# Staged weight loads, gathers and weight pieces put in another order between attention and the experts

## The chip, the cores and the metric

One core of a Trainium2 chip runs the whole program. The metric is device time in microseconds (us) of one execution; smaller is better. The time of the kernel before is the median of three runs.

Five engines work side by side[...]: TensorE (PE in the profile, PEld for its weight loads), VectorE (DVE), ScalarE (ACT), GpSimd (POOL) and SyncE (SP). SyncE and ScalarE issue plain DMA transfers here; GpSimd issues the indirect ones (gathers and scatters by a list of row numbers) and those that convert fp32 to fp16 on the way.

## The reference

Two layers, one behind the other. The first is causal linear attention with decay, in blocks of 64 positions, for 4 batches x 8 heads x 768 positions x 64. Its output is the input of the second, seen as 3072 tokens of 512 numbers. The second sends each token to the one of 8 experts whose embedding is nearest to it by cosine.

```python
xn = x / (np.linalg.norm(x, axis=-1, keepdims=True) + 1e-06)
en = expert_emb / (np.linalg.norm(expert_emb, axis=-1, keepdims=True) + 1e-06)
logits = xn @ en.T / tau
expert_idx = np.argmax(logits, axis=1)
...
for e in range(E):
    mask = expert_idx == e
    h = np.maximum(x[mask] @ w1[e], 0.0)            # [n, 512] @ [512, 1024]
    out[mask] = gate_w[mask, None] * (h @ w2[e])    # [n, 1024] @ [1024, 512]
```

`gate_w` is the softmax probability of the chosen expert. Each expert has 4 MB of fp32 weights, so the experts together read 32 MB.

## The kernel before

**Attention** runs in 24 blocks of 128 tokens, `for i in range(1, R)`. As blocks finish, they are routed in seven groups: of four blocks each for the first five, then of two. A routed group is written row by row to a table in DRAM, `x_dram`, by `write_x`. From the routing the kernel makes lists of the rows of each *region*. Regions 0 and 1 hold the first tokens (those of the first 16 blocks) of experts 0 and 1, regions 2 and 3 the rest of these two, regions 4 to 9 all tokens of experts 2 to 7. A region has 1, 2 or 3 full tiles of 128 tokens and a half tile of 64; the half tiles of two neighbouring regions share one gather, called `("h", r)`.

**The experts.** For each tile of a region the rows are gathered from `x_dram` to `x_e` by GpSimd, transposed by PE into PSUM (`xtr`), and copied to `xTe` by ScalarE. `pe_L1(r)` computes the hidden layer of region r in 8 groups of four matmuls, each followed by a relu on ScalarE. `pe_L2(r, g)` computes the output of one tile in eight matmuls (`pe_L2h(r)` that of two half tiles), and `put` scales it by the gate on VectorE and scatters it to the output by an indirect DMA.

```python
        def pe_xT(r, g0, g1):
            xt_copy(r, g0, g1, ps_mx.tile([P, DC * P * (g1 - g0)], FP16, name="xtr", tag="xtr"))
        ...
        def put(y_ps, r, g):
            y = moe_y.tile([P, DM], FP32, name="y_sb", tag="y_sb")
            nc.vector.tensor_scalar(y, y_ps, xe[r][:, g, DW : DW + 1].bitcast(FP32), None,
                                    op0=ALU.mult)
            nc.gpsimd.indirect_dma_start(
                out=out_views[n_scat[0]],
                ...)
            for x in after.get(n_scat[0], []):
                ...                       # the gathers of later regions, in a fixed order
            if n_scat[0] > 1:
                part_cast()
            n_scat[0] += 1
```

**The weights** come in two ways. Those of experts 0 to 2 come in twelve pieces that GpSimd's DMA converts to fp16 (`load_w`; 512 KB each as written, 1 MB as read). Those of experts 3 to 7 come in 40 *parts* of 512 KB of fp32: SyncE loads a part into one of four staging tiles (`w_st`), VectorE casts it to fp16 into the weight tile, and the next load starts into the tile that came free.

```python
        def part_load():
            if at_part[0] < len(parts):
                ...
                t = wst.tile([P, F], FP32, name="w_st", tag="w_st")
                nc.sync.dma_start(t, ...)
                staged.append(t)

        def part_cast():
            at_part[2] += 1
            if at_part[1] < len(parts) and at_part[2] % 5:
                ...
                nc.vector.tensor_copy(w..., staged.pop(0))
                part_load()
```

`part_cast` is called at fixed places: in `put` from the third output tile on, and inside `pe_L1`:

```python
            nc.scalar.activation(hT[r][:, fc, 0:n], h_ps[:, 0:n], AF.Relu)
            if r > 0 and fc % (4 if n < P * 2 else 2) == 1:
                part_cast()
```

Every fifth call does nothing. `n` is 320 tokens for regions 0 and 1, 192 for 2 and 3, and 448 for the others, so a hidden layer of region 1 or of 4 to 9 has four such calls, one of 2 or 3 has two.

**The hand-over.** In the attention loop, gathers and weight pieces are issued on GpSimd at the end of block i:

```python
    for i, r, g in ((19, 0, 0), (19, 0, 1), (20, ("h", 0), 0), (20, 1, 0), (20, 1, 1)):
        at(i, "g", gather, r, g)
    for i in (7, 9, 11, 13, 15, 19, 19, 20, 20, 21, 21, 21):
        at(i, "g", load_w, 1)
```

The first gathers need the row writes of the first four groups, that of the fourth (`write_x(3)`) being issued by ScalarE in block 19. After the last block:

```python
        write_x(GL)
        pe_L1(0, range(4, 8))
        for _ in range(4):
            part_load()
        for gi in range(GL - 2, GL + 1):
            pe_list(gi, kaz[:, 320:384], first=(gi == GL - 2), last=(gi == GL))
        ev_list(GL)
        ids(ES, NR)
        gather(2, 0)
        gather(3, 0)
        gather(pairs.pop(0), 0)
        rt_b2(GL)
        pe_L2(0, 0)
        pe_L2(0, 1)
        pe_L1(1)
        pe_L2h(0)
        pe_xT(2, 0, 1)
        pe_L2(1, 0)
        pe_xTh(2)
        pe_L2(1, 1)
        pe_L1(2)
        pe_xT(3, 0, 1)
        pe_L2(2, 0)
        pe_xT(4, 0, 2)
        pe_L1(3)
        pe_xT(4, 2, 3)
        pe_L2h(2)
        pe_xTh(4)
        pe_L2(3, 0)
        for r in range(2 * ES, NR, 2):
            ...                           # regions 4 to 9
```

Of the kernel before, what the change touches and what calls it, by code (L numbers as in the profile page):

```python
# [20 lines left out]
def kernel(  # L21
# [13 lines left out]
    P = 128  # L35
# [56 lines left out]
    moe_t1 = ctx.enter_context(tc.tile_pool(name="moe_t1", bufs=2))  # L92
    moe_h1 = ctx.enter_context(tc.tile_pool(name="moe_h1", bufs=1))
# [589 lines left out]

    todo = {}

    def at(i, slot, fn, *a):
        todo.setdefault((i, slot), []).append((fn, a))
# [26 lines left out]
    for i, r, g in ((19, 0, 0), (19, 0, 1), (20, ("h", 0), 0), (20, 1, 0), (20, 1, 1)):  # L714
        at(i, "g", gather, r, g)
    for i in (7, 9, 11, 13, 15, 19, 19, 20, 20, 21, 21, 21):
        at(i, "g", load_w, 1)

# [92 lines left out]
    def pe_L1(r, fcs=range(FC), early=()):  # L811
# [6 lines left out]
        for k, fc in enumerate(fcs):  # L818
            if early:
                h_ps = ps.tile([P, 512], FP32, name="s_h", tag=early[k])  # L820
            else:
                h_ps = ps_h.tile([P, 512], FP32, name="h_ps", tag="h")
            for c in range(DC):
                nc.tensor.matmul(h_ps[:, 0:n], w_chunk(w, c, fc), xTe[r][:, c, 0:n],  # L824
                                 start=(c == 0), stop=(c == DC - 1))
            nc.scalar.activation(hT[r][:, fc, 0:n], h_ps[:, 0:n], AF.Relu)  # L826
            if r > 0 and fc % (4 if n < P * 2 else 2) == 1:
                part_cast()
# [13 lines left out]
    with (  # L842
# [5 lines left out]
        tc.tile_pool(name="wst", bufs=4) as wst,  # L848
# [15 lines left out]

        parts = [(e, which, c) for e in range(3, E) for which in (1, 2) for c in range(DC)]
        staged = []
        at_part = [0, 0, 0]

        def part_load():
            if at_part[0] < len(parts):  # L870
                e, which, c = parts[at_part[0]]
                at_part[0] += 1
                t = wst.tile([P, F], FP32, name="w_st", tag="w_st")
                nc.sync.dma_start(t, w1_r[e][:, c, :] if which == 1
                                  else w2_r[e][:, c].rearrange("p s d -> p (s d)"))
                staged.append(t)

        def part_cast():
            at_part[2] += 1
            if at_part[1] < len(parts) and at_part[2] % 5:  # L880
                e, which, c = parts[at_part[1]]
                at_part[1] += 1
                w_alloc(e)
                w = w_tiles[(e, which)]
                nc.vector.tensor_copy(w[:, c, :] if which == 1  # L885
                                      else w[:, 2 * c : 2 * c + 2, :].rearrange("p s d -> p (s d)"),
                                      staged.pop(0))
                part_load()

        pairs = [("h", r) for r in range(ES, NR, 2)]  # L890

        def pe_xT(r, g0, g1):
            xt_copy(r, g0, g1, ps_mx.tile([P, DC * P * (g1 - g0)], FP16, name="xtr", tag="xtr"))

        def pe_xTh(r):
            xth_copy(r, ps_mx.tile([P, DC * P], FP16, name="xtr_h", tag="xtr"))

        def put(y_ps, r, g):
            y = moe_y.tile([P, DM], FP32, name="y_sb", tag="y_sb")
            nc.vector.tensor_scalar(y, y_ps, xe[r][:, g, DW : DW + 1].bitcast(FP32), None,  # L900
                                    op0=ALU.mult)
# [16 lines left out]
            if n_scat[0] == n_out - 8:  # L918
                nc.gpsimd.drain()
# [55 lines left out]
        for _ in range(4):  # L975
            part_load()
# [4 lines left out]
        gather(2, 0)  # L981
        gather(3, 0)
        gather(pairs.pop(0), 0)
# [4 lines left out]
        pe_L2h(0)  # L988
        pe_xT(2, 0, 1)
        pe_L2(1, 0)  # L990
        pe_xTh(2)
        pe_L2(1, 1)
        pe_L1(2)
        pe_xT(3, 0, 1)
# [138 lines left out]
```

## Time and profile before

| | |
|---|---|
| median of three runs | 259.68 us (259.17 to 264.58) |
| the profiled run | 264.65 us, of which 263.0 us are the program's span |
| busy share of the span | PE 92%, VectorE 53%, GpSimd 52%, ScalarE 47% |
| moved by DMA | 60.33 MB, mean 229 GB/s |

The profile gives for each engine when it worked, and for each idle time what ended it. A line of a group or of the timeline names the source line (L824), the engine, the operation, and the tiles as output<-input. L824 are the matmuls of the hidden layers, L826 the relus, L925 and L934 the matmuls of the output layers, L900 and L902 the scaling and the scatter of an output tile, L653 the gathers, L666 the transposes of gathered rows, L874 and L885 the staged load of a part and its cast, L321 and L323 the weight pieces of GpSimd, L462 the row writes. "x_e<-x_dram,lid" is a gather of a full tile, "x_e<-x_dram,lh" one of half tiles. A wait for several things is put down to the one that came last by the profile.

In the span, attention runs to about 133 us and the experts from 135 us to 257 us.

### The profile page before, as it was taken

To read this page: it belongs to the slowest core of one execution; us is meant where nothing else is said; L and a number is where in the kernel's file an instruction comes from. 1 tells how busy PE (TensorE), PEld (TensorE's weight loads), DVE (VectorE), ACT (ScalarE), POOL (GpSimd) and SP (SyncE) were. 2 spreads that over 40 slices of the span, in tenths; PEclk is the share of its full clock that TensorE was granted. 3 is DMA by queue.
4 is the path that set the end of the run, shared out by engine and by line. 5 is a ranking of instruction groups with operands and counts; after the bars stand their busy time and mean duration, and the time that the engine had idled before them with its cause. 6 is when DMAs were issued, how large, how long until landed. Compare 5 with 4: busy or idle time off the path is not lost. (4 is left out here: it accounts for less than half of the span.)

```text
span 263.0 us, 7404 instructions
## 1 busy us (share of the span) xinstructions
PE 241.4 (92%) x3011; PEld 166.8 (63%) x3012; DVE 139.1 (53%) x353; ACT 123.2 (47%) x277; POOL 137.2 (52%) x191
## 2 busy tenths in 40 slices
PE   7989999999999999989999864799999999999990
PEld 3777898897887987967855423475555555455440
DVE  1554677577667667846756524036554544554031
ACT  4745564653564555534573411355454436353600
POOL 7653436449236736269940877037274837440541
PEclk9999999999999999999999979599999999999997
DMA  7999999999999999339999999467898999982321
GB/s 152 238 223 231 238 207 228 253 242 196 210 198 249 228 229 238 85 61 216 198 226 270 340 358 337 182 196 215 327 319 303 310 393 332 306 284 90 128 83 57
DMA packets 79542, 60.33 MB, mean 229 GB/s; under 512 B 54504, under 2 KB 68840, under 8 KB 79506
## 3 DMA queue, kind: packets, MB, share of 16 engines
q1 hardware_dynamic: 71440, 42.51, 59.7%
q0 software_dynamic: 6976, 16.63, 26.2%
q10 hardware_dynamic: 1090, 0.70, 1.2%
q8 instruction: 24, 0.39, 0.6%
q14 instruction: 12, 0.10, 0.2%
HBM read 56.48 MB, written 10.94 MB: 256 GB/s over the span
## 5 line engine op out<-in xcount | busy, mean ns | idle before, releaser
L824 PE MATMUL h_ps<-xTe,w_sb 128*128 128x448 f16 (+2 forms) x312 | 52.6, 324 | 5.9 <-ACT hT L826 4.4
L826 ACT ACTIVATE hT<-h_ps 128x448 f16<-128x448 f32 (+2 forms) x78 | 36.9, 481 | 43.3 <-PE h_ps L824 27.3
L900 DVE TENSOR_SCALAR y_sb<-y_ps,x_e 128x512 f32<-128x512 f32 x29 | 21.7, 750 | 51.8 <-PE y_ps L925 22.8
L339 POOL TENSOR_TENSOR ks<-kn,kdec 128x512 f32<-128x512 f32 (+1 forms) x25 | 25.2, 1008 | 45.6 <-issue 20.7
L824 PEld LDWEIGHTS <-w_sb 128*128 128x128 f16 x320 | 30.6, 99 | 27.7 <-issue 7.4
L925 PE MATMUL y_ps<-w_sb,hT 128*128 128x512 f16 x192 | 47.3, 399 | 0.0
L392 DVE TENSOR_TENSOR stm<-s_ps,step 128x512 f32<-128x512 f32 x48 | 30.9, 686 | 26.4 <-PE s_ps L384 23.0
L902 POOL DMA_INDIRECT out_dram<-y_sb,lid x24 | 26.0, 1085 | 34.4 <-DVE y_sb L900 29.5
L653 POOL DMA_INDIRECT x_e<-x_dram,lid x24 | 26.2, 1092 | 16.3 <-PE h_ps L824 8.2
L885 DVE CAST w_sb<-w_st 128x1024 f16<-128x1024 f32 x40 | 27.5, 712 | 12.4 <-DMA w_st<-in_moe_w_dram 11.9
L925 PEld LDWEIGHTS <-hT 128*128 128x128 f16 x192 | 18.9, 102 | 21.2 <-issue 3.7
L384 PE MATMUL s_ps<-qT,kT 64*64 64x128 f32 x768 | 27.4, 276 | 0.9 <-issue 0.6
L415 PE MATMUL o_ps<-stm,vn 128*64 128x128 f32 x384 | 26.8, 279 | 0.2 <-issue 0.2
L456 ACT ACTIVATE sq<-xps 128x512 f16<-128x512 f32 x24 | 14.3, 598 | 24.3 <-PE xps L454 23.0
L384 PEld LDWEIGHTS s_ps<-qT,kT 64*64 64x64 f32 x768 | 21.2, 132 | 7.0 <-issue 5.3
L415 PEld LDWEIGHTS o_ps<-stm,vn 128*64 128x64 f32 x384 | 20.5, 136 | 3.1 <-issue 2.6
L424 ACT COPY xT<-o_ps 128x256 f32<-128x256 f32 x24 | 8.9, 373 | 28.1 <-PE o_ps L415 28.1
L360 DVE TENSOR_TENSOR qT<-q_ps,lamq 128x512 f32<-128x512 f32 x22 | 15.1, 687 | 3.5 <-PE q_ps L354 3.2
L674 ACT COPY xTe<-xtr 128x512 f16<-128x512 f16 (+1 forms) x14 | 10.8, 768 | 11.7 <-PE xtr L666 8.7
L370 PE MATMUL k_ps<-ident,ks 128*128 128x128 f32 x96 | 14.8, 275 | 0.8 <-POOL ks L339 0.7
L586 POOL TENSOR_SCALAR l_row<-lrow,hl 128x128 f16<-128x128 f32 x22 | 13.3, 603 | 4.1 <-DVE hl L547 3.8
L372 ACT COPY kT<-k_ps 128x512 f32<-128x512 f32 x24 | 14.4, 598 | 2.1 <-PE k_ps L370 2.1
(148 smaller groups left out, 335.9 us busy)
## 6 DMA issues: line engine op xcount, KB each, us to landing
w_st<-in_moe_w_dram SPq DMA_DIRECT2D x40, 512.0 KB
vn<-in_v_dram SPq DMA_DIRECT2D x24, 256.0 KB
w_sb<-in_moe_w_dram POOLq DMA_DIRECT2D x12, 512.0 KB
kn<-in_k_dram SPq DMA_DIRECT2D x23, 256.0 KB
qn<-in_q_dram SPq DMA_DIRECT2D x11, 512.0 KB
x_dram<-xg SPq DMA_DIRECT2D x8, 272.0 KB
x_dram<-xg ACTq DMA_DIRECT2D x2, 272.0 KB
x_dram<-xg SPq DMA_DIRECT2D x4, 136.0 KB
```

The lines of the kernel that those rows point to most:

```text
L339: nc.gpsimd.tensor_tensor(ks[i][:, h : h + n], kn[i][:, h : h + n], kdec[:, i % RB, h : h + n].unsqueeze(2).to_broadcast([P, n, D]), op=AL ...
L360: nc.vector.tensor_tensor(qT[j][:, :, :, s, :].rearrange("p a h i -> p h a i"), t.rearrange("p h (a i) -> p h a i", i=64), lamq[:, j % NC, ...
L384: nc.tensor.matmul(bank["s", h2][ds(64 * m, 64), hp, :], kT[i][ds(64 * h2, 64), hp, ds(64 * m, 64)], q_of(i, hp)[ds(64 * h2, 64)], start=( ...
L392: nc.vector.tensor_tensor(stm[i][:, h2], bank.pop(("s", h2)), step.unsqueeze(1).to_broadcast([P, HP, P]), op=ALU.mult)
L415: nc.tensor.matmul(bank["o", h2][ds(64 * u, 64), b2, :], vn[i][:, 2 * hp + h2, :], stm[i][:, h2, hp, :], start=(i % RB == 0 and b2 == 0), ...
L653: nc.gpsimd.indirect_dma_start(out=xe[r][:, g, :], out_offset=None, in_=x_dram[0 : TA * P] if first else x_dram[:], in_offset=bass.Indirec ...
L824: nc.tensor.matmul(h_ps[:, 0:n], w_chunk(w, c, fc), xTe[r][:, c, 0:n], start=(c == 0), stop=(c == DC - 1))
L826: nc.scalar.activation(hT[r][:, fc, 0:n], h_ps[:, 0:n], AF.Relu)
L885: nc.vector.tensor_copy(w[:, c, :] if which == 1 else w[:, 2 * c : 2 * c + 2, :].rearrange("p s d -> p (s d)"), staged.pop(0))
L900: nc.vector.tensor_scalar(y, y_ps, xe[r][:, g, DW : DW + 1].bitcast(FP32), None, op0=ALU.mult)
L902: nc.gpsimd.indirect_dma_start(out=out_views[n_scat[0]], out_offset=bass.IndirectOffsetOnAxis(ap=idl[r][:, 1, g : g + 1], axis=0), in_=y[: ...
L925: nc.tensor.matmul(y_ps, hT[r][:, fc, ds(col0(r) + P * g, P)], w[:, fc, :], start=(fc == 0), stop=(fc == FC - 1))
```

## The change

It reorders what shares the DMA engines around the hand-over, so that the gathers of the second regions (2 and 3) don't run beside weights, and uses the stretch in which little is moved:

- The first four staged loads go to the end of attention block 18. A memset of one column of each staging tile on VectorE holds them back until there: SyncE has to wait for it. The pool of staging tiles is made at the start of the kernel for that.
- The first half-tile gather goes from block 20 to block 19, and only five weight pieces are issued in blocks 20 and 21, instead of seven in blocks 19 to 21. The last two, of expert 2's second layer, are issued after the gathers of regions 2 and 3. These gathers come in the order region 2, half tiles, region 3.
- Region 1's hidden layer has no casts any more (`r > 1`), so that no further staged load starts before the third output tile.
- PE's order changes: the first output tile of region 1 comes before the transposes of region 2, and all transposes of regions 2 and 3 before the hidden layer of region 2.
- The transposes go by turns to two PSUM banks instead of one (`xt_bank`).
- The last output tile is scaled half by VectorE and half by ScalarE, and GpSimd's drain comes when seven output tiles are left instead of eight.

```diff
+    wst = ctx.enter_context(tc.tile_pool(name="wst", bufs=4))
...
+    def part_load():
+        if at_part[0] < len(parts):
...
+            t = wst.tile([P, F], FP32, name="w_st", tag="w_st")
+            if len(staged) < 4 and at_part[0] <= 4:
+
+                nc.vector.memset(t[:, 0:1], 0.0)
+            nc.sync.dma_start(t, w1_r[e][:, c, :] if which == 1
+                              else w2_r[e][:, c].rearrange("p s d -> p (s d)"))
+            staged.append(t)
...
-    for i, r, g in ((19, 0, 0), (19, 0, 1), (20, ("h", 0), 0), (20, 1, 0), (20, 1, 1)):
+    for i, r, g in ((19, 0, 0), (19, 0, 1), (19, ("h", 0), 0), (20, 1, 0), (20, 1, 1)):
         at(i, "g", gather, r, g)
-    for i in (7, 9, 11, 13, 15, 19, 19, 20, 20, 21, 21, 21):
+    for i in (7, 9, 11, 13, 15, 20, 20, 20, 21, 21):
         at(i, "g", load_w, 1)
+
+    for _ in range(4):
+        at(18, "end", part_load)
...
-            if r > 0 and fc % (4 if n < P * 2 else 2) == 1:
+            if r > 1 and fc % (4 if n < P * 2 else 2) == 1:
                 part_cast()
...
+        n_xt = [0]
+
+        def xt_bank(n):
+            n_xt[0] += 1
+            if n_xt[0] % 2:
+                return ps_mx.tile([P, n], FP16, name="xtr", tag="xtr")
+            return ps2.tile([P, n], FP16, name="xtr2", tag="xps")
...
+            gate = xe[r][:, g, DW : DW + 1].bitcast(FP32)
+            if n_scat[0] == n_out - 1:
+                nc.vector.tensor_scalar(y[:, 0 : DM // 2], y_ps[:, 0 : DM // 2], gate, None, op0=ALU.mult)
+                nc.scalar.activation(y[:, DM // 2 :], y_ps[:, DM // 2 :], AF.Copy, scale=gate)
+            else:
+                nc.vector.tensor_scalar(y, y_ps, gate, None, op0=ALU.mult)
...
-            if n_scat[0] == n_out - 8:
+            if n_scat[0] == n_out - 7:
                 nc.gpsimd.drain()
...
         pe_L1(0, range(4, 8))
-        for _ in range(4):
-            part_load()
...
         gather(2, 0)
+        gather(pairs.pop(0), 0)
         gather(3, 0)
-        gather(pairs.pop(0), 0)
+        load_w(2)
         rt_b2(GL)
         pe_L2(0, 0)
         pe_L2(0, 1)
         pe_L1(1)
         pe_L2h(0)
+        pe_L2(1, 0)
         pe_xT(2, 0, 1)
-        pe_L2(1, 0)
+        pe_L2(1, 1)
         pe_xTh(2)
-        pe_L2(1, 1)
+        pe_xT(3, 0, 1)
         pe_L1(2)
-        pe_xT(3, 0, 1)
         pe_L2(2, 0)
```

## The prediction

> **What bounds the kernel now.** I read the page's slices first. Slice n begins at n x 6.575 us. TensorE (PE) is at 9 tenths nearly everywhere but in slices 22 to 25 (145 to 171 us), the hand-over from attention to the experts; there alone its clock falls too. DMA is full from slice 18 on, with two holes: slices 16 and 17 (105 to 118 us) and 25 to 27.
>
> ```profile
> PE   7989999999999999989999864799999999999990
> ...
> PEclk9999999999999999999999979599999999999997
> DMA  7999999999999999339999999467898999982321
> ```
>
> So outside the hand-over the matmuls are the limit, and a microsecond saved inside it reaches the end if the stages behind can follow. The second view is busy time by windows (window, its length, busy us of PE, PEld, DVE, ACT, POOL with counts, granted clock, DMA share, GB/s).
>
> ```profile
> 152.00:154.00 2.00, 0.46 (x3) 0.00 (x0) 1.35 (x2) 0.00 (x0) 1.69 (x2) 1.00 0.90 266
> ...
> 156.00:158.00 2.00, 2.00 (x6) 0.72 (x5) 0.00 (x0) 0.00 (x0) 1.67 (x2) 0.51 1.02 416
> ...
> 162.00:164.00 2.00, 0.24 (x3) 0.24 (x3) 0.00 (x0) 0.33 (x1) 1.39 (x3) 1.00 0.89 325
> ...
> 168.00:170.00 2.00, 2.00 (x6) 0.76 (x5) 0.00 (x0) 0.46 (x1) 0.00 (x0) 0.50 0.05 21
> ```
>
> PE loses time in two ways, idle and at half clock. The third view, the timeline of this stretch, says which waits (start, duration, what, and in brackets the idle time before it and who ended it).
>
> ```profile
> 144.55 1.31 POOL L653 DMA_INDIRECT x_e<-x_dram,lid  x1 [8.22 <-PE h_ps L824]
> ...
> 147.50 1.05 POOL L653 DMA_INDIRECT x_e<-x_dram,lh  x1 [0.30 <-issue]
> ...
> 154.51 0.60 PE L666 MATMUL xtr_h<-ident,x_e 128*128 128x128 f16 x4 [2.05 <-DMA x_e<-x_dram,lh]
> ...
> 163.37 0.33 ACT L826 ACTIVATE hT<-h_ps 128x192 f16<-128x192 f32 x1 [3.24 <-remote]
> ...
> 163.75 0.49 PE L824 MATMUL h_ps<-xTe,w_sb 128*128 128x192 f16 x4 [3.08 <-ACT hT L826]
> ```
>
> The gather of region 2 starts at 144.55 although its list was ready at 140.8: the matmul named was long done, so what it waited for is the last row write (issued 139.41). That write shares the DMA engines with the tail of seven SWDGE weight pieces (share 1.11 over 130 to 140 us) and, from 140.73, with the first four staged loads. The gather then needs 5.8 us until PE starts on it (144.55 to 150.33, where PE waited 1.1 us for it), that of the half tiles 7.0 us (147.50 to 154.5), because L1(1)'s four casts have released four more 512 KB loads. PE idles, and runs at half clock after it. The third stall (160.7 to 166.2) is different: relus of L1(2) wait 3.2, 1.1 and 1.1 us for products whose matmuls were recorded earlier.
>
> [...] 0.51 and 0.50 above, and eight 512-column matmuls take 3.41 us from 154.90 against 1.89 at 150.57. [...]
>
> **The change, part by part.**
>
> *Four staged loads move* from 140.73 into the hole at 105 to 118 us. A memset behind block 18's router step (VectorE, done about 106.7) holds them until then. At 364 GB/s, the rate of 144.5 to 150 us, a 512 KB load takes 0.524/0.364 = 1.44 us, so four fill 5.8 us of a hole with share 0.35. They overlap the fourth group's row writes (issued 107.92, 108.64; the first gather waits for them until 113.47). I allow the gather 0 to 2 us of delay. Its transposes start at 119.29, and the tile waited for no DMA then; the two weight pieces that came between the first gathers are now behind them. Effect on the end: 0 to +1 us.
>
> *Weight pieces:* five instead of seven before the hand-over. Seven pieces ran from 117 to 140, some 3.2 us each beside the row writes, so five end about 6 us earlier and the last row write meets a freer DMA. I put the gather of region 2 at 142 to 143 instead of 144.55. The order is now region 2, half tiles, region 3, then the two pieces: half tiles at 144 to 145 instead of 147.50.
>
> *No casts in L1(1)* (r > 1), so no staged load starts before the third row-block eviction (about 150). The gathers have DMA to themselves; I give them 3 us instead of 5.8 to 7.
>
> *PE order:* L2(1,0) before xT(2), xT(3) before L1(2), transposes in two PSUM banks. From L2h(0) at 147.3 (full-clock durations from the timeline): L2h(0) 1.92 + L2(1,0), L2(1,1), L2(2,0) 3 x 1.89 + xT(2), xTh, xT(3) 3 x 0.40 + L1(2) 3.3 (as L1(3), 171.77 to 175.07) + xT(4,0:2) 0.61 = 12.7 us. ScalarE's two half copies before L1(2), 0.65, make 13.4. L1(3) would start at 160.7; it starts at 171.75 now. **That is 11 us to be had in the profiled run.** Data is there in time: region 2 is needed at 151.1 (landed by 146), half tiles at 153.4 (by 148), region 4's first two at 159.5. Those last come behind two pieces and two scatters at some 1.35 us per GpSimd issue, so about 151, plus 7 us at worst.
>
> *Last eviction split* over VectorE and ScalarE: half of 0.75, some 0.3 us off the tail.
>
> **How much of the 11 us the timed runs hold.** The profiled run took 264.65 us, the median of three 259.68. So 5 us of the profile are not in a median run. The third stall is the only one of about that size whose cause the trace doesn't show (160.7 to 166.2, plus half clock behind it); I assume that it is mostly what the median lacks. Then 11 - 5 = 6 us remain to be won; if the 5 us lie elsewhere, 11.
>
> **Can DMA follow?** It is the candidate for the next bound.
>
> ```profile
> 180.00:240.00 60.00, 60.00 (x365) 31.06 (x364) 30.16 (x49) 30.33 (x54) 30.63 (x33) 1.00 0.91 311
> 147.30:240.00 92.70, 83.98 (x526) 45.11 (x526) 41.21 (x65) 39.48 (x79) 47.92 (x49) 0.94 0.86 295
> ```
>
> From 147.3 to 240 DMA works 92.7 x 0.86 = 79.7 us. After the change one staged load fewer is left then (36 instead of 37: -1.4) and two SWDGE pieces more (+6.4): 84.7 us. At the 0.91 of the steady stretch this takes 93 us and ends at 146 + 93 = 239; at 0.97 it ends at 233. The last cast (240.9 now) is needed at L2h(8), 249.1 now and 238 after an 11 us shift. So loads and matmuls finish close together: casts come later against PE (four chances lost in L1(1), so the fortieth falls into L1(9) instead of before it), and VectorE, which also empties y_ps, will sometimes wait for w_st. I take 0 to 3 us for it, 1 in the middle.
>
> Sum for the median run: 259.7 - 6 (or up to -11) + 0.5 (attention) - 0.3 (tail) + 1 (loads). With the smaller saving 254.9, with the larger 249.9; at weights of about 0.6 and 0.4, **253.0 us**.
>
> **Rivals.** (a) Loads become the bound: the steady share of 0.91 and 8.8 us of casts waiting for w_st after 171.7 speak for it, PE's 60.00 of 60.00 in the same stretch against it: today's waits cost PE nothing. Then 255 to 258. (b) The early loads hold back the fourth group's row writes, thus the first gathers and the transposes in block 21, and attention stalls: for it, both use all DMA engines from 107 on; against it, 6 us between gather and use. Costs 1 to 3 us, so 254 to 256. (c) The third stall stays in L1(2), as its cause is open: DMA shares near 1 beside it speak for that, the lighter loads in the new order against it. Then 257 or so. (d) All goes well and the median has the whole 11 us: 249.
>
> **Range and chances.** 2% is 254.5. The middle of my sum lies 1.5 us below it, (a) and (c) lie above, (d) far below. Range 248.5 to 258.5. Faster by over 2%: 0.64; within 2%: 0.32; slower: 0.04, as no part adds more than 3 us to a path that loses at least 3.
>
> **What would show it.** Four w_st loads between 106 and 116; the gather of region 2 before 143.5 and PE on it without a DMA wait; clock 1.0 from 145 to 175 and PE busy above 22 of 24.5 us after L2h(0) starts; L1(3) within 15 us of L2h(0). Wrong if the first early transposes wait for x_e, if PE idles for h_ps or y_ps between 165 and 235 behind casts that wait for w_st, or if L2h(8) waits for the last cast.

## The result and the profile after

The changed kernel takes **263.06 us** (median of 4 runs, 262.27 to 267.16), the kernel before, run beside it, 261.69 us (4 runs, 259.17 to 264.58). The ratio is **1.013, 95% interval 1.0095 to 1.0165**: slower by 1.3%. The prediction had 253.0 us and a range of 248.5 to 258.5. Ratios here leave out disturbed executions of both kernels, so a ratio need not equal the quotient of two medians; each profile is of one execution, that of the changed kernel of its slowest (267.16 us) and that of run 4 below likewise (256.39 us).

The slices of the page, changed kernel (one slice is 6.635 us):

```profile
PE   7999999999999999975999995789999999999990
...
PEclk9999999999999999996899999559999999999996
DMA  7998999999899999764997189955979999999221
```

DMA's hole in slices 16 and 17 is partly filled (7 and 6 tenths instead of 3 and 3), as planned, but slice 18 (119 to 126 us), full before, is at 4 now, and slice 22 at 1. The dip of TensorE (PE) in the hand-over is still there (slices 24 to 26, 159 to 179 us), and in slices 17 and 18 there is a new one, with the clock down in 18 and 19. The windows show both, and the steady stretch (window, its length, busy us of PE, PEld, DVE, ACT, POOL with counts, granted clock, DMA share, GB/s):

```profile
113.00:118.00 5.00, 5.00 (x101) 4.70 (x101) 3.51 (x10) 1.77 (x5) 0.00 (x0) 1.00 0.86 279
118.00:121.00 3.00, 0.06 (x3) 0.00 (x0) 1.33 (x7) 1.27 (x4) 2.20 (x2) 1.00 0.19 49
121.00:124.00 3.00, 1.76 (x20) 1.30 (x24) 0.00 (x0) 0.50 (x1) 2.13 (x3) 0.53 0.37 89
124.00:128.00 4.00, 4.00 (x62) 3.67 (x56) 1.29 (x2) 0.88 (x2) 4.00 (x5) 0.50 0.67 116
...
165.00:168.00 3.00, 0.84 (x7) 0.58 (x8) 0.75 (x1) 0.00 (x0) 2.39 (x3) 0.59 1.03 416
168.00:172.00 4.00, 3.74 (x24) 3.13 (x23) 0.69 (x1) 1.58 (x3) 3.08 (x4) 0.50 1.04 414
...
180.00:240.00 60.00, 60.00 (x361) 30.90 (x359) 31.58 (x50) 29.34 (x54) 31.79 (x35) 1.00 0.90 305
```

From 118 to 121 PE does next to nothing, at a DMA share of 0.19; in the kernel before it is busy for all of these 3 us:

```profile
118.00:121.00 3.00, 3.00 (x50) 2.62 (x50) 1.55 (x5) 1.65 (x4) 2.39 (x3) 1.00 0.98 181
```

From 121 to 128 PE runs at half clock in the changed kernel. The same pair, a gap and then half clock, stands at 163 to 179. From 180 to 240 PE is busy all the time, as before. The timeline of the changed kernel names what ended each gap:

```profile
118.45 1.18 POOL L654 DMA_INDIRECT x_e<-x_dram,lid  x1 [6.30 <-DVE t L538]
...
121.52 0.61 PE L667 MATMUL q_xtr<-ident,x_e 128*128 128x128 f16 x4 [3.46 <-DMA x_e<-x_dram,lid]
...
149.09 1.19 POOL L654 DMA_INDIRECT x_e<-x_dram,lid  x1 [8.61 <-PE h_ps L857]
...
152.90 1.57 POOL L324 DMA_DIRECT2D w_sb<-in_moe_w_dram  x2
...
157.79 1.05 POOL L654 DMA_INDIRECT x_e<-x_dram,lid  x1 [0.30 <-issue]
159.15 1.06 POOL L654 DMA_INDIRECT x_e<-x_dram,lid  x1 [0.30 <-issue]
...
166.94 0.61 PE L667 MATMUL xtr<-ident,x_e 128*128 128x128 f16 x4 [3.83 <-DMA x_e<-x_dram,lid]
```

and in the kernel before, for the first of them:

```profile
113.47 1.18 POOL L653 DMA_INDIRECT x_e<-x_dram,lid  x1 [1.40 <-DMA x_dram<-xg]
...
119.31 0.61 PE L666 MATMUL q_xtr<-ident,x_e 128*128 128x128 f16 x8
```

The first gather comes 5.0 us later (118.45 against 113.47), and the first early transposes wait 3.46 us for it. At 166.94 region 4's transposes wait 3.83 us for rows whose gathers stand behind the two late weight pieces of 152.90.

### The profile page after: what moved, and what is told of

The parts are those of the page before. It is cut to its first block, busy times and chain, and to the rows that moved or that the text cites. A ratio compares the mean times of both kernels' runs of the same rounds, so it can differ in the third digit from the quotient of the medians.

```text
span 265.4 us, 7415 instructions
## 1 busy us (share of the span) xinstructions
PE 243.3 (92%) x3011; PEld 169.8 (64%) x3012; DVE 139.9 (53%) x357; ACT 123.5 (47%) x278; POOL 136.5 (51%) x191
## 5 line engine op out<-in xcount | busy, mean ns | idle before, releaser
L857 PE MATMUL h_ps<-xTe,w_sb 128*128 128x448 f16 (+2 forms) x312 | 54.6, 333 | 3.0 <-ACT hT L859 1.4
L857 PEld LDWEIGHTS <-w_sb 128*128 128x128 f16 x320 | 32.2, 103 | 25.1 <-issue 4.7
L919 DVE TENSOR_SCALAR y_sb<-y_ps,x_e 128x512 f32<-128x512 f32 x28 | 21.0, 751 | 46.1 <-PE y_ps L952 28.1
L943 PE MATMUL y_ps<-w_sb,hT 128*128 128x512 f16 x192 | 44.1, 379 | 0.0
L654 POOL DMA_INDIRECT x_e<-x_dram,lid x24 | 25.6, 1067 | 21.6 <-PE h_ps L857 8.6
L708 DVE CAST w_sb<-w_st 128x1024 f16<-128x1024 f32 x40 | 28.1, 724 | 15.0 <-DMA w_st<-in_moe_w_dram 15.0
L943 PEld LDWEIGHTS <-hT 128*128 128x128 f16 x192 | 18.0, 98 | 19.7 <-issue 0.8
L457 ACT ACTIVATE sq<-xps 128x512 f16<-128x512 f32 x24 | 14.3, 598 | 23.5 <-PE xps L455 22.2
L416 PEld LDWEIGHTS o_ps<-stm,vn 128*64 128x64 f32 x384 | 21.2, 140 | 2.7 <-issue 2.1
L667 PEld LDWEIGHTS <-x_e 128*128 128x128 f16 x116 | 8.2, 104 | 13.4 <-DMA x_e<-x_dram,lid 9.3
```

Of the source, the lines that this page charges most:

```text
L416: nc.tensor.matmul(bank["o", h2][ds(64 * u, 64), b2, :], vn[i][:, 2 * hp + h2, :], stm[i][:, h2, hp, :], start=(i % RB == 0 and b2 == 0), ...
L654: nc.gpsimd.indirect_dma_start(out=xe[r][:, g, :], out_offset=None, in_=x_dram[0 : TA * P] if first else x_dram[:], in_offset=bass.Indirec ...
L708: nc.vector.tensor_copy(w[:, c, :] if which == 1 else w[:, 2 * c : 2 * c + 2, :].rearrange("p s d -> p (s d)"), staged.pop(0))
L919: nc.vector.tensor_scalar(y, y_ps, gate, None, op0=ALU.mult)
L943: nc.tensor.matmul(y_ps, hT[r][:, fc, ds(col0(r) + P * g, P)], w[:, fc, :], start=(fc == 0), stop=(fc == FC - 1))
```

## The experiments

Three marks split every trace: the first matmul of region 0's hidden layer ("attention end"), from there to the first relu of region 4 ("hand-over"), and from there to the end ("rest").

| version (run) | attention end | hand-over | rest | ratio to before |
|---|---|---|---|---|
| before, first profile | 132.2 | 47.9 | 83.0 | |
| before, second profile (8) | 136.2 | 39.3 | 82.6 | |
| **changed kernel** | 136.4 | 46.2 | 82.8 | 1.013 [1.0095, 1.0165] |
| early loads undone (1) | 129.5 | 44.2 | 82.6 | 1.0004 [0.9968, 1.0040] |
| late pieces undone (3) | 135.7 | 37.0 | 82.6 | 1.0044 [1.0019, 1.0069] |
| both undone (4) | 132.5 | 39.4 | 82.8 | **0.9888 [0.9803, 0.9973]** |
| before + early loads (2) | 137.4 | 37.7 | 82.6 | 1.0103 [1.0019, 1.0188] |
| pieces behind first gathers (10) | 129.9 | 42.0 | 82.5 | **0.9881 [0.9841, 0.9921]** |

The rest lies between 82.3 and 83.0 us in all profiles but those of runs 7, 9 and 15 (86.8, 83.9 and 83.4). Run 4's execution was 2.2 us late before any of this: its fourth group's row writes were issued at 110.2 us, those of run 1 at 108.0.

**My theory after the result** was that the change holds two faults, one each side of the hand-over: the early loads hold back the fourth group's row writes, and the late pieces stand in front of region 4's gathers. The rivals were that only one of them counts, or that PE's new order, the second transpose bank or the loads in the end phase are at fault.

### Undoing one part at a time (runs 1 to 4)

Run 1, the staged loads back behind the last row write:

```diff
-    for _ in range(4):
-        at(18, "end", part_load)
...
         pe_L1(0, range(4, 8))
+        for _ in range(4):
+            part_load()
```

> The changed kernel with its four first staged loads back behind the last block, all else as changed. Queue theory (the loads stand in front of the fourth group's row writes and cost attention 4.2 us): the row writes run 109 to 112 again, the first gather starts near 113.5 instead of 118.5, attention ends 4 us earlier; time about 258.5, against 262.8 for the changed kernel in its undisturbed runs. Rival, weights bound the end (the early loads buy the lead that the fewer casts cost): attention gains 4 us and the end loses them again to casts that wait for w_st; time 261.5 or more.

Run 2, the kernel before with the early loads alone:

> The kernel before, with only the four staged loads moved to block 18. Queue theory: first gather at 118, attention 4 us longer, and of these at most 1 comes back because the hand-over has 2 MB less to move; time 262.5 to 263.5 against 259.4 for the kernel before in its undisturbed runs. Rival, loads bound the end: the lead of four loads and the free DMA at 141 give the 4 us back; 259 to 260.

Run 3, the changed kernel with all seven pieces back ahead of the hand-over:

```diff
-    for i in (7, 9, 11, 13, 15, 20, 20, 20, 21, 21):
+    for i in (7, 9, 11, 13, 15, 19, 19, 20, 20, 21, 21, 21):
...
-        load_w(2)
```

> The changed kernel with seven weight pieces in blocks 19 to 21 and none behind the gathers of regions 2 and 3; staged loads still early. Queue theory (one GpSimd queue, worked off in order: two pieces hold the gathers of region 4 by 4 us): PE waits for region 4's gather under 0.5 us instead of 4, no half clock behind it; against that the seven pieces start at 120 and end at 145, so the last row write comes 2 to 4 us later; time 258 to 261. Rival, the slow hidden layer of region 3 is the cost and comes by itself: 262.8, unchanged.

Run 4, both undone, the rest of the change kept:

> The changed kernel with both the staged loads and the weight pieces back in their old places: what is left is the half-tile gather in block 19, no casts in region 1's hidden layer, PE's new order, two PSUM banks, the split last eviction. Queue theory: attention ends as before, region 4's gather in time, PE idles under 2 us between region 0's output and region 3's hidden layer; 254 to 256. Rival, weights bound the end: 258.5 or more, with casts waiting for w_st over 15 us in all and PE idle behind them after 190 us.

Medians: 256.36, 259.15, 257.28 and 253.82 us, before on the same chip 257.13. Beside run 4, the early loads alone (run 3) cost 1.0044/0.9888 = 1.016, the late pieces alone (run 1) 1.0004/0.9888 = 1.012. Run 4 had four executions, so both costs are known only roughly: with the intervals of both ratios, 0.7 to 2.5% for the early loads and 0.2 to 2.1% for the late pieces. Both on top of run 4 make 0.9888 x 1.0158 x 1.0117 = 1.016, against the measured 1.013. So each counts, the two add up within this uncertainty, and what is left of the change is worth 1.1%. The changed kernel itself was not run again beside these four; its 1.013 comes from another set of executions (there the kernel before took 261.69 us, here 257.13). Early loads in the old kernel (run 2) cost 1.0%.

The page does not show where the row writes go, but the trace's records of single transfers do. Read off for the fourth group's two writes (issued by ScalarE at 107.9 to 109.0; 512 packets of 1088 B):

```
                         first packet   last one ends   first gather
before                      109.25         112.22          113.47
early loads undone (1)      109.32         112.43          113.67
two early loads (5)         112.15         115.58          116.97
changed kernel (four)       112.70         117.27          118.45
```

In the changed kernel the first write is issued 1.1 us after the first of SyncE's four loads (106.89), and the writes hardly move until the loads have nearly run out, though the two go through different queues (the loads on q1, the writes on q10 of the profile's list): by 114 us 36 of the 512 write packets have started, and the last load packet ends at 115.98. In all four kernels the first gather starts 1.2 to 1.4 us after the last write packet, so it is the writes that it waits for, also at 118.45, where the profile names VectorE. No row-write packet starts for 4.7 us after the issue of the first write (108.01 to 112.70), against 1.3 us in the kernel before, which does not look like even sharing (the alternative in run 5's expectation below, with writes that start at once and only run slower); whether the writes' packets stood ready in that time the trace does not show, so why they came late stays open.

What the delay costs can be read off whole. From 117 us to the end of attention PE is busy for 15.22 of 19.40 us in the changed kernel and for 12.31 of 12.50 us in run 1. The idle 4.2 us are waits for gathered rows (3.46 and 0.72 us); the longer busy time comes with the 6.83 us at half clock behind them. Together, 4.0 us more idle and 2.9 us more busy are the 6.9 us between the two attention ends. The hand-over gives a part back (37.0 us in run 3, 39.4 in run 4, in single profiles), which leaves some 4.5 us, near the 4.1 that 1.6% are.

### The late pieces and the queue of GpSimd (runs 1, 4 to 7)

In run 4, with no pieces behind the gathers, region 4's rows cost PE 1.34 us, and the chain from region 0's half tile (L934 before, L946 here) runs as the prediction added it up:

```profile
150.41 1.92 PE L946 MATMUL y_ps<-w_sb,hT 128*64 128x512 f16 x16
...
156.79 2.81 PE L851 MATMUL h_ps<-xTe,w_sb 128*128 128x192 f16 x32 [0.24 <-ACT xTe L681]
159.44 1.89 PE L937 MATMUL y_ps<-w_sb,hT 128*128 128x512 f16 x8
...
162.90 0.40 PE L667 MATMUL xtr<-ident,x_e 128*128 128x128 f16 x4 [1.34 <-DMA x_e<-x_dram,lid]
163.13 1.15 PE L851 MATMUL h_ps<-xTe,w_sb 128*128 128x192 f16 x12
```

In run 1, with the late pieces, the same wait is longer than in the changed kernel:

```profile
152.14 1.25 POOL L654 DMA_INDIRECT x_e<-x_dram,lid  x1 [0.30 <-issue]
153.69 1.06 POOL L654 DMA_INDIRECT x_e<-x_dram,lid  x1 [0.30 <-issue]
...
162.31 1.30 PE L667 MATMUL xtr<-ident,x_e 128*128 128x128 f16 x8 [5.21 <-DMA x_e<-x_dram,lid]
```

The packets say why. In the changed kernel the packets of the two pieces of 152.90 run from 154.4 to 163.1, those of the two scatters of 154.77 and 156.23 begin at 162.2, and those of region 4's gathers, issued at 157.79 and 159.15, at 164.5. All three kinds are on one queue of the profile (q0), and in this trace they start in the order of their issue, whatever they are for. With pieces in front, PE gets a gather's rows 9.1 us after its issue (changed kernel) or 10.2 us (run 1); without them it takes 5.9 to 6.5 us (the gathers that PE waits for in runs 3, 4, 7 and 9).

Runs 5 to 7 vary both faults: run 5 has two early loads instead of four, run 6 four loads held until block 19's gathers are issued, by a memset on GpSimd instead of VectorE, run 7 is run 6 with the two pieces behind region 4's gathers:

```diff
-                nc.vector.memset(t[:, 0:1], 0.0)
+                nc.gpsimd.memset(t[:, 0:1], 0.0)
...
-        at(18, "end", part_load)
+        at(19, "g", part_load)
...                                                   # run 7 only:
+            if n_scat[0] == 2:
+                load_w(2)
...
-        load_w(2)
```

> The changed kernel with two of the four early loads kept at block 18 and two back behind the last block. If row writes stand in line behind all loads issued before them (queue theory), half the loads cost half the delay: row-write packets start near 110.5 (112.7 with four, 109.3 with none), first gather near 116, and since the early transposes come at 118 to 119, PE waits for them 0 to 1 us instead of 4.2 and keeps its full clock: ratio to the kernel before 0.999 to 1.005, near that without early loads (1.000), not half way to 1.013. If the engines share evenly between queues instead, the row writes would start at once, as soon as issued, and only run slower.

> The changed kernel with the four early loads held until GpSimd has issued the three first gathers (a memset on GpSimd instead of VectorE), in block 19. Queue theory: row writes and the three gathers as without early loads (first gather 113.5, no PE wait for it), loads from 117 on in front of the weight pieces; the pieces still hold region 4's gathers, so PE still waits 4 us there and falls to half clock: ratio 0.995 to 1.002. Rival, any loads between 106 and 120 cost attention: ratio 1.01 as with the early loads.

> As the run before, and the last two weight pieces go behind the gathers of region 4 (third output tile) instead of in front of them. Queue theory: both head-of-line blocks are gone, no PE gap over 1.5 us from the last attention block to region 4, clock above 0.99; ratio 0.980 to 0.988, at least as good as with everything put back (0.989). Rival, weights bound the end: the pieces arrive too late for region 4's output (PE waits for w_sb at its first output tile) or the casts fall behind, ratio 0.995 or more.

Run 5: 260.12 us, ratio 1.0154 [1.0067, 1.0240], a miss. Halving the loads saved 1.5 us of the gather's delay and nothing in time that the interval shows. The delay is not halved: the first write packet comes at 112.15 and not at 110.5, when the two loads (last packet 112.32) have all but ended. Run 6: 261.34 us, 1.0210 [1.0112, 1.0309], also a miss; the row writes ran as in the kernel before and attention ended at 129.9, but region 4's rows came still later:

```profile
166.96 1.26 PE L667 MATMUL xtr<-ident,x_e 128*128 128x128 f16 x8 [8.58 <-DMA x_e<-x_dram,lid]
```

Run 7: 257.19 us, 1.0004 [0.9962, 1.0047], short of the 0.980 to 0.988 that was expected; the hand-over fell from run 6's 47.1 to 39.0 us, and the rest rose from 82.3 to 86.8. There the loss only moved on: the pieces now stand in front of region 5's gathers, PE waits 2.1 us for those rows at 176.0, and 3.4 us at half clock follow. So where the pieces stand in GpSimd's queue, and not how many bytes the kernel moves in all, makes the loss.

### The kernel before a second time (run 8)

> The kernel before, unchanged, for another look at it. The first profile had 5 us more than the median and a slow hidden layer of region 2 (relus 1.1 to 3.6 us apart, PE at half clock before and after). If that stretch is what comes and goes, it now takes 3 to 4 us like that of region 3, the clock is 0.98 or above and region 0's half tiles to region 4's hidden layer take 20 to 25 us instead of 29.7. If it is a fixed part of the kernel, 29 us again.

```profile
118.00 1.06 POOL L653 DMA_INDIRECT x_e<-x_dram,lh  x1 [0.30 <-DVE qT L360]
...
125.52 0.61 PE L666 MATMUL k_xtr<-ident,x_e 128*128 128x128 f16 x4 [2.93 <-DMA x_e<-x_dram,lh]
```

259.19 us (two executions), the profiled one with a span of 258.1. The ratio of this kernel to itself came out at 1.0111 [0.9990, 1.0233]: from so few executions a single 1% is not told from noise. Its hand-over takes 39.3 us instead of 47.9: the relus of L1(2) come every 0.33 us and not, as in the first profile, up to 3.6 us apart. From L2h(0) to L1(3), the output of region 0's half tile to the hidden layer of region 3, it is 16.05 us (151.19 to 167.24) and not 24.4. Its attention is longer by 4 us: the half-tile gather of 118.00 stands behind two weight pieces, PE waits 2.93 us, and 124.5 to 134.7 run at half clock. That is a wait which the change really removes.

### Better places for the pieces and the loads (runs 9, 10, 12)

Seven pieces all behind the five first gathers; staged loads behind region 3's gather (run 9) or at their old place (run 10); and in the kernel before the same places for gathers and pieces alone (run 12):

```diff
-    for i in (7, 9, 11, 13, 15, 20, 20, 20, 21, 21):
+    for i in (7, 9, 11, 13, 15, 20, 20, 20, 21, 21, 21, 21):
...
-        load_w(2)
```

> The changed kernel, but all seven weight pieces go behind the five first gathers (three in block 20, four in 21), none behind those of regions 2 and 3, and the four first staged loads go behind region 3's gather. Gap theory (the time is that of PE, plus its gaps, plus half clock behind them; the rest from region 4 on is a constant 82.6 us): attention ends at 129.5 as in the runs without early loads, and from there to region 4's first relu it takes 37 to 38 us as in the run with pieces and loads both early; span 249 to 250, time 250.5 to 252.5, ratio 0.975 to 0.985. Rival, loads this late bound the end: casts wait for w_st and the part from region 4 on grows over 84 us; ratio 0.99 or more.

> As the run before, but the four staged loads start behind the last block, as in the kernel before, and so run beside the last row write and the gathers of regions 2 and 3. If four loads there cost the 2 us that the runs with them show more than those without (39.4 against 37.3 from attention's end to region 4's first relu), the ratio is 0.005 to 0.01 above the run before. If not, equal.

> The kernel before with one thing of the change: the five first gathers go in front of the weight pieces (half-tile gather in block 19, pieces three in block 20 and four in 21). If the half-tile gather behind two pieces is what stops attention in the kernel before (2.9 us of PE wait and up to 10 us at half clock in its second profile), attention ends at 129.5 to 130 and the ratio is 0.98 to 0.99, most of what the best version has. If that gap is an accident of one profile, 1.00.

Run 9: 254.92 us, 0.9885 [0.9839, 0.9932], a little above the expected 0.975 to 0.985. Run 10: 254.91 us, 0.9881 [0.9841, 0.9921]. Both beat both kernels, as run 4 does; the place of the staged loads between these two makes no difference. Run 12: 257.85 us, 1.0036 [1.0004, 1.0068], a miss in time, though attention ends at 130.0 as expected. In its profile (span 255.3) the marks are hardly different from run 10's (130.0, 42.4, 82.8), but PE waits 2.92 us for the half tiles and needs 15.6 us from L2h(0) to L1(3), where run 9 needs 12.5. So I take the new order of PE and of the gathers to be what runs 4, 9 and 10 gain by. That is argued and not shown: no run undid it alone, nor parted it from the missing casts of region 1, the second PSUM bank and the split last eviction, which these runs keep too.

### The attention's second loss (runs 11, 14, 16)

If the early transposes only wait for late rows, moving them one block later should hide that (run 11):

```diff
-    at(R - 3, "pe2", early_xT, 0)
+    at(R - 2, "pe2", early_xT, 0)
```

> The changed kernel as it is, but the early transposes of region 0 come one block later (22 instead of 21). The staged loads still delay the row writes and the first gather still starts near 118.5. If the early loads cost time only through PE's wait for that gather and the half clock behind it, the wait and the 6.8 us at half clock are gone: attention ends near 130 instead of 136.4, ratio 0.99 to 1.000 (the gap at region 4's gathers stays). If loads beside row writes cost attention in another way, the ratio stays at 1.01.

264.94 us, 1.0255 [1.0210, 1.0299]: a clear miss, and slower than the changed kernel. Waits from 117 to 141 us (engine, tile, line, what it waited for: us in total, times, longest):

```profile
PE q_xtr L667 <- ACT zT L477: 6.9, 1, 6.9
...
DVE nrm L564 <- POOL nrm L514: 6.2, 1, 6.2
...
ACT xg L458 <- POOL xg L452: 5.3, 1, 5.3
```

PE no longer waits for rows but for ScalarE, and this for a memset of the row group `xg`, which stands on GpSimd behind the gathers, these waiting for the row writes, and behind three pieces and the norm of the fifth group. Run 14 moves the memset to VectorE, run 16 instead moves the norm ahead of block 20's gathers:

```diff
-            nc.gpsimd.memset(xg[gi][:, :, DW:], 0)          # run 14
+            nc.vector.memset(xg[gi][:, :, DW:], 0)
...
-        at(n, "pool", rt_n, gi)                             # run 16
+        at(n, "end", rt_n, gi)
```

> The changed kernel with the first early transposes one block later (as in the eleventh run), and the memset of the row group's last words on VectorE instead of GpSimd. If GpSimd's queue, with its gathers waiting for the row writes in front of that memset, is what kept ScalarE and TensorE waiting for 7 us there, that wait goes, the attention ends about 4 us earlier than in the eleventh run (136 instead of 140) and the ratio is 1.00 to 1.012 instead of 1.0255. If the norm behind it on GpSimd, or the row writes themselves, are the cause, it stays within 0.6% of 1.0255.

> The eleventh run's kernel (the changed kernel, first early transposes one block later) with the norm of the fifth row group issued on GpSimd ahead of block 20's gathers and pieces instead of behind them. There VectorE waited 6.2 us for that norm and TensorE 6.9 us behind it. If the norm's place in GpSimd's order is the cause, that TensorE wait falls below 3 us, the attention ends at 133 to 137 us instead of 140.3, ratio 1.00 to 1.015. If the gathers of block 19, which wait for the row writes, still stand in front of it (they do: about 4 us of the delay), the norm comes only 4 to 5 us earlier and some wait stays. If neither, it stays at 1.0255.

Run 14: 266.49 us, 1.0385 [1.0218, 1.0552], so wide that run 11's value lies in it; attention ends at 140.5 as in run 11 (140.3). The wait passed on to the norm:

```profile
126.71 1.10 POOL L514 TENSOR_TENSOR nrm<-nsq_all,half 128x4 f32<-128x4 f32 x1
127.84 0.65 DVE L564 TENSOR_SCALAR nrm<-nrm 128x4 f32<-128x4 f32 x1 [6.26 <-POOL nrm L514]
128.99 0.23 ACT L570 ACTIVATE pe<-dz 128x32 f32<-128x32 f32 x1 [5.91 <-DVE dz L567]
...
129.53 1.01 PE L667 MATMUL q_xtr<-ident,x_e 128*128 128x128 f16 x8 [7.43 <-ACT zT L477]
```

Run 16: median 266.45 us beside 263.34 for the kernel before on that chip, without an interval. The norm now runs at 121.85 instead of 126.91, attention ends at 137.65, and PE's wait is 4.65 us and not below 3, this time behind the memset again:

```profile
127.64 0.23 POOL L452 MEMSET xg<- 128x64 int32 x1
127.90 0.58 ACT L458 CAST xg<-xps 128x512 f16<-128x512 f32 x1 [3.12 <-POOL xg L452]
...
128.93 1.01 PE L667 MATMUL q_xtr<-ident,x_e 128*128 128x128 f16 x8 [4.65 <-ACT zT L477]
```

So two small instructions, 0.2 and 1.1 us long, stand one beside the other in GpSimd's order; with either out of the way the other still holds ScalarE. Both at once was not tried. GpSimd's stream, late by the 5 us of its first gather, is thus a second way in which early loads can reach PE. In the changed kernel itself it costs nothing: there PE's waits for rows and the half clock behind them are the whole 6.9 us.

### Pieces ahead of the second regions' gathers, and the norm moved in the better versions (runs 13, 15, 17, 18)

Runs 13 and 15 put the two late pieces behind the last block's norm, with the staged loads at their old place (13) or behind region 3's gather (15). Runs 17 and 18 are runs 9 and 10 with the norm moved as in run 16.

```diff
         rt_n(GL)
+        load_w(2)
...
         gather(3, 0)
-        load_w(2)
```

> The changed kernel with its staged loads back behind the last attention block and the last two weight pieces issued right behind the norm of the last block, so ahead of the gathers of regions 2 and 3; five pieces stay behind the first gathers. Theory (GpSimd queue worked off in order, each TensorE gap paid once more at half clock): pieces are through before region 2's gather is issued, so region 4's gathers wait for nothing; the attention ends at about 129.5 us as in the undone early loads, the stretch to region 4's first relu takes 37 to 40 us, the rest 82.6: ratio 0.975 to 0.985. Rival (the two pieces beside the last row write hold it and region 2's gather back): stretch 42 us or more, ratio 0.99 to 1.00.

> The first kernel of this call, with the four staged loads held until region 3's gather is issued. If staged loads beside the last row write and region 2's gather cost time (some 2 us between two earlier runs), the stretch to region 4's first relu is 1 to 3 us shorter than in the first kernel of this call, ratio 0.97 to 0.98. If not, it is the same within 0.3%, or 1 us longer through casts that come later.

> The ninth run's kernel (pieces behind the first gathers, staged loads behind region 3's gather) with the same move of the norm. If the norm behind the pieces is what keeps VectorE (2.2 us) and ScalarE (3.0 us) waiting in block 21 there and opens TensorE's gap of 2.4 us before the last block, the gap and the half clock behind it go: last row write 1 to 2.5 us earlier, 1 to 3 us less in all, 252 to 254 us, ratio 0.978 to 0.986. If list making on GpSimd, which stays behind the pieces, is the limit: within 0.3% of the ninth run.

> The tenth run's kernel (pieces behind the first gathers, staged loads at their old place) with the same move of the norm: same two readings as for the kernel before it in this call, 252 to 254.5 us or unchanged at 254.9.

Runs 13 and 15: 254.79 and 255.23 us (before: 257.39), ratios 0.9949 [0.9910, 0.9988] and 0.9965 [0.9939, 0.9992]: slightly faster than before, and no better than run 10. The rival of run 13 holds. Attention ends at 129.35, but the last row write, issued at 137.9 as in run 1, lets region 2's gather go only at 145.8 against 142.97 there: it runs beside the two pieces, as the windows of run 13 and then of run 1 show.

```profile
138.00:146.00 8.00, 8.00 (x52) 4.72 (x52) 3.10 (x12) 3.50 (x9) 0.20 (x1) 1.00 1.09 292
```

```profile
138.00:143.00 5.00, 5.00 (x32) 2.65 (x29) 3.10 (x12) 1.13 (x3) 0.03 (x1) 1.00 0.73 212
```

Runs 17 and 18: 265.21 and 262.57 us on a chip where the kernel before took 263.34, ratios 1.0013 [0.9973, 1.0054] and 1.0004 [0.9976, 1.0032]. Both missed: attention ended later (135.3 and 133.6 against 129.6 and 129.9). In run 18 PE waits for VectorE in block 19 already, 2.36 us at 118.5, half clock follows, and L1(2) is slow as in the first profile of before. Moving the norm gained nothing here; runs 9 and 10 were not repeated on that chip, so what the move itself costs is not parted from what the chip does.

## Why the prediction was wrong

**What bounds the kernel**: right. The rest takes 82.3 to 83.9 us in all profiles but run 7's, and in the changed kernel PE is busy for 60.00 of 60.00 us from 180 to 240; what is lost or won before shows up at the end. Rival (a), loads become the bound, falls with that for the changed kernel. Only where the staged loads start as late as region 3's gather (runs 9 and 15) does PE wait for VectorE in the rest, 1.1 and 1.0 us.

**The early loads**: the step that failed first. "I allow the gather 0 to 2 us of delay", "Effect on the end: 0 to +1 us" was an allowance without a sum behind it. It took the hole by its mean, "a hole with share 0.35". But the row writes run just there: in the kernel before the share is 0.13 from 105 to 109 us, 0.79 from 109 to 112 and 0.02 from 112.3 to 115. The loads did not fill a hole, they were put in front of the writes. Measured: the gather comes 5.0 us later, attention ends 136.4 instead of 129.5 us (changed kernel against run 1), and undoing them in the changed kernel moves the ratio from 1.013 to 1.0004. Rival (b) named the mechanism and had it too small (1 to 3 us), as it left out the half clock behind the wait, 2.9 of the 6.9 us, and counted the slack too high. That "both use all DMA engines" was shown only as a mean over the 16: 0.79 with the writes in the kernel before (109 to 112 us), 0.86 with loads and writes in the changed kernel (113 to 118 us). The "6 us between gather and use" that I held against it were 5.84 (113.47 to 119.31), but the rows themselves need 3.1 of them (118.45 to 121.52 in the changed kernel), so some 2.8 us were slack, and the delay is 5.0; as PE was also through with its other work 1.25 us sooner (118.06 against 119.31), it waited 3.46.

**The late pieces**: the second step that failed. "Those last come behind two pieces and two scatters at some 1.35 us per GpSimd issue, so about 151, plus 7 us at worst" counted issue time on GpSimd, and 7 us for all transfers in its queue. The issue came at 157.79, late above all because region 2's gather was (149.09), and the rows at 166.9: 9.1 us after it. With the early loads undone (run 1) the issue came at 152.14, near the 151, and the rows 10.2 us after it, with 5.21 us of PE wait; so the transfer of the pieces in front is the term that was too small. Cost: 1.2% (run 1 against run 4). The chance of 0.04 for slower rested on "no part adds more than 3 us to a path that loses at least 3": the early loads cost 1.6%, 4.1 us, the late pieces 1.2%, 3.0 us, and the path lost 1.1%, 2.8 us.

**Region 2's gather by 143.5**: wrong. It came at 149.09, because the last row write was issued only at 143.55. That write took its own 5.1 to 5.5 us from issue to gather in before (139.41 to 144.55), the second profile (143.3 to 148.7) and the changed kernel, although the DMA share was only 0.24 from 144.5 to 150. It was not the seven pieces' tail. In run 13, with two pieces beside it and a share of 1.09, it took 7.9 us. Where the forecast time was met, as in run 1 (142.97), it was luck: the write was as long (5.07 us) and only issued earlier.

**PE's order**: right as a sum. The prediction had 12.7 to 13.4 us from L2h(0) to L1(3); with both faults undone it is 12.7 (run 4) and with pieces early 12.4 (run 3), against 16.7 in the changed kernel.

**"That is 11 us to be had", of which 6 remain for the median**: mis-sized. The second profile of before has 16.05 us there, and the old order took 14.3 us in run 2 and 15.6 in run 12, so the ordinary gain is 1.6 to 3.4 us (16.05 - 12.7); 24.4 - 16.05 = 8.4 us belonged to the first profile alone, where I took 5. That agrees with the 1.1 to 1.2% that runs 4 and 10 win, some 3 us. Rival (c) is not borne out as a fixed part: L1(2) is slow in some profiles of several kernels and not in others.

With the measured terms the sum is: order and gathers -1.1%, early loads +1.6%, late pieces +1.2%, together +1.7%, where +1.3% (0.95 to 1.65%) was measured. All three terms rest on run 4, so this shows that they add up and not that each is exact.

**What the evidence for it would be**: four staged loads between 106 and 116 came true. Of the signs against it one came true: the first early transposes waited for x_e (3.46 us). PE also stood idle at 163 to 167, but behind a gather and not, as named, behind casts. The split last eviction (-0.3 us) drowns in the rest's spread.

**What stays open**: why ScalarE's row writes hardly move beside loads on SyncE's queue (36 of 512 packets started by 114 us); why L1(2) runs slowly in some profiles; and which part of what run 4 keeps of the change wins its 1.1%.

## What to carry to other kernels

A stretch with a low mean DMA share can hold something short and critical (here row writes, at a share of 0.79 from 109 to 112 us, in a hole put at 0.35): before filling the stretch, split it into shorter windows, look at what is issued just behind the new loads and who waits for it, and count the delay through to the end of the loads. All that GpSimd was given here, gathers, weight pieces, memsets and small vector work, came out in its order (region 4's rows 9.1 us after the issue of their gather behind two pieces, 5.9 to 6.5 us without), so a bulk transfer goes behind the last gather that is needed soon, not just behind the one that it was in the way of (run 7). Take a second profile before a stall is taken for a part of every run.

## What was not expected of the hardware

- Row writes on ScalarE's queue, issued 1.1 us after the first of four 512 KB loads on SyncE's, had their first packet 4.7 us after their issue instead of 1.3; with two loads still 3.9 us (108.24 to 112.15).
- PE gaps of the same length had different prices in half clock: none after 2.92 us in run 12, 10.2 us of it with the 2.93 us in the second profile of before, 13.7 us with the 3.83 us at 166.94 in the changed kernel, 6.8 us with the 3.46 us at 121.52 there, and 3.4 and 6.8 us with the 2.05 and 3.08 us in the first profile of before. Before the last output tiles the stretches at half clock lasted 3.41 and 6.83 us in the first profile of before and 6.83 and 13.65 us in the changed kernel, and the one from 124.5 us in the second profile of before 10.2 us: one, two, three or four times 3.41 us.
- L1(2) of run 18 gave a relu every 1.43 us for work that takes 0.33 to 0.5, partly at full clock (0.83 in the mean from 159 to 164 us), with nothing in the profile that PE waits for:

```profile
162.14 0.49 PE L851 MATMUL h_ps<-xTe,w_sb 128*128 128x192 f16 x4 [1.60 <-issue]
...
163.57 0.49 PE L851 MATMUL h_ps<-xTe,w_sb 128*128 128x192 f16 x4 [0.94 <-issue]
```
